# Four early loads of v asked for at other points, with a new list of priority offsets, in a gated linear attention followed by a four-expert layer

## The chip, the core and the metric

The kernel runs on one core of a Trainium2 chip. Its engines are TensorE (PE in the profile; PEld is its weight load), VectorE (DVE), ScalarE (ACT), GpSimd (POOL) and SyncE (SP). SP and POOL also ask for DMA transfers, and the core's 16 DMA engines carry them. The metric is device time in microseconds (us) of one execution, as a median of several runs.

## The reference

Two stages. The first is a linear attention with a forget gate: for each of 4 batches and 8 heads a 48 x 48 state is decayed and updated over 768 steps, and read with q. The second takes the 3072 rows of 384 numbers that come out and runs four experts over all of them, each a 384 -> 1024 -> 384 layer with relu, weighted by normalised probabilities.

```python
f = 1.0 / (1.0 + np.exp(-f_logit))
for t in range(S):                                   # S = 768
    state = f[:, :, t, :, None] * state + np.einsum('bhd,bhe->bhde', k[:, :, t], v[:, :, t])
    y[:, :, t] = np.einsum('bhd,bhde->bhe', q[:, :, t], state)
x = y.transpose(0, 2, 1, 3).reshape(3072, 384)
p = probs / (probs.sum(-1, keepdims=True) + 1e-09)
for e in range(4):
    out += p[:, e:e + 1] * (np.maximum(x @ w1[e], 0.0) @ w2[e])
```

## The kernel before

**Tiling.** The 768 steps are cut into six chunks c of 128 steps. A chunk has four batches b. For each (c, b) the attention part runs these steps, which carry these names in the kernel's planner: `ld f`, `ld k`, `ld q`, `ld v` (loads from HBM), `gate1`, `gate2` (ACT: log of the gate), `cs` (PE: running sum of it over the 128 steps, line 319), `exps` (ACT, line 339), `q` and `k` (products with the exponentials on DVE or POOL, line 347), `tpq`, `tpk` (transposes on PE for the first batches, line 356; DMA transposes `tp`, line 360, later), `ev_tp` (eviction of those), `at` (PE, line 383), `ev_at0`, `ev_at1` (DVE, masked eviction, line 387), `y` (PE, lines 394 and 398; needs v), then `ev_y`, `xt`, `ev_xt` in the first chunk and part of the second (eviction, transpose on PE, eviction: x ready for the experts), or `ev_ys` (ACT or DVE, lines 370 and 372: the eviction scaled by two experts' probabilities) and the DMA transpose `xs` (line 375) later. `kv`, `ev_kv` and `sf` (lines 404, 411, 416, 419) update the state.

The expert part of chunk 0 and half of chunk 1 is written plainly: `h c.e.fc` (PE, x times w1, line 432), `relu`, `o` (PE, h times w2, line 447), `ev_o`. From the second half of chunk 1 on, two experts and two batches make one group c.hf.p: eight `hs` steps (PE, line 464), their `relu_s`, four sums `s1` to `s4` (DVE, line 482), and seven products `p` (PE, line 501) in place of eight, each with its eviction `ev_p` (DVE or ACT, line 509). `store` writes the output.

**Order.** Nothing is scheduled by a compiler. Every step is put into a planner (`Plan`, line 53) with the engines that could run it and a cost there, a due time (`prio`), what it depends on, and the buffers that it takes and frees. The planner lays the steps out with a list scheduler, and the instructions of each engine are emitted in that order; each engine then runs its list strictly in order. `MOVES` (line 15) is a list of offsets that are added to the due times of single steps, with `@DVE` or `@ACT` where a step is tied to one engine. Before the first expert matmul the planner also puts idle matmuls on a tile of ones (`pad`, line 867) between PE's steps, as many as its plan has room for.

**The first loads.** The sixteen loads of chunk 0 are one batch each. f, k and q go through SP's queue (line 282). v is asked for by POOL (line 278), since its load also casts to bf16. POOL's list in this stretch also holds one or more of the `q` and `k` products and the eleven loads of the experts' weights (`w issue`, line 291). w 0 and w 1 are the two halves of w1 of expert 0, w 2 and w 3 those of expert 1, w 4 and w 5 the halves of w2 of expert 0, and w 6 to w 10 whole matrices. A v issue can be gated: `after` (line 258) makes it wait until a given load has landed. `v_gate` names the gates, and the planner is told the same dependency:

```python
    v_gate, issued = [(0, "k", 1), (0, "k", 2)], []
...
    for i, x in enumerate("f0 k0 q0 f1 k1 q1 f2 f3 k2 q2 v0 k3 q3 v1 v2".split()):
```

The string sets the due times of the loads on the DMA engines; v 0.3 is added behind the first weight load. So before the change v 0.0 waits for k 0.1, v 0.1 waits for k 0.2, and v 0.2 and v 0.3 follow in POOL's list without a gate.

Of the kernel before, what the change touches and what calls it, by code (L numbers as in the profile page):

```python
# [12 lines left out]


MOVES = (
    "q 0.2=3.2;k 0.3=-8.9;ev_y 0.3=-23.3@ACT;cs 1.0=0.8;k 1.0=-0.2;cs 1.1=-4.4;v 1.2=8@ACT;tp 1.2=-43.6;tp 1.3=-25;ev_xt 1.1=24.3;"
    "xs 1.3.1=7.9;ld v2.2=7.4;h 0.0.0.0=-7.3;relu 0.0.0.0=3.1@DVE;relu 0.0.2.0=10.6;relu 0.0.3.0=29@ACT;h 0.0.5.0=6.8;h 0.1.1.0=-16.7;"
    "h 0.1.2.0=-22.6;h 0.1.3.0=-119.1;o 0.1.1.1=4.2;o 0.1.3.0=11.3;h 0.3.2.0=-3.7;relu 0.3.3.0=-13.8@DVE;h 0.3.4.0=-12.9;o 0.2.2.0=28.6;"
    "o 0.2.3.0=-1.9;h 0.3.7.0=39.5;cs 2.1=31.3;tp 2.2=9.1;ev_at1 2.0=17;ev_ys 2.0.0.1=-0@ACT;ev_ys 2.1.1.0=-35.5@ACT;xs 2.1.1=12.6;"
    "ev_ys 2.2.0.1=-0.6@ACT;kv 2.2=48.1;ld k3.0=-2.9;o 0.3.2.1=2.1;store 0.3.0=22.7;h 1.0.0.0=-9.5;relu 1.0.4.0=-0.8@DVE;"  # L20
    "h 1.0.5.0=-42.9;h 1.1.0.0=-50.1;h 1.1.1.0=-41.2;h 1.1.2.0=-4;relu 1.1.2.0=-12.9@DVE;h 1.1.3.0=-41;h 1.1.4.0=-2.3;"
    "relu 1.1.6.0=-44.9@DVE;h 1.2.0.0=-1.9;h 1.2.1.0=-7.4;h 1.2.3.0=-7.1;relu 1.2.4.0=1.6@DVE;h 1.2.5.0=8.6;h 1.3.2.0=8;o 1.2.1.0=10.2;"
    "h 1.3.4.0=-11.3;h 1.3.5.0=-23.7;h 1.3.6.0=-11.9;hs 1.1.0.1.4=-1.2;relu_s 1.1.0.1.4=-9@ACT;hs 1.1.0.1.6=-6.4;hs 1.1.1.1.4=4.8;"
    "exps 3.0=7.9;k 3.1=-3.6;k 3.2=56.5;ev_ys 3.0.0.0=-1.5@DVE;ev_ys 3.0.0.1=0@ACT;ev_ys 3.0.1.0=44.9;ev_ys 3.1.0.0=50.8@DVE;"
    "ev_ys 3.1.0.1=0@ACT;ev_at1 3.2=7.6;ev_ys 3.3.1.0=0.1@DVE;ev_ys 3.3.1.1=6.1@DVE;ev_kv 3.0=23;kv 3.3=9.3;ev_kv 3.3=13.2;"
    "ld q4.0=-11.2;ld k4.2=26.7;ld q4.2=26.5;ev_p 1.1.1.1=6.4;hs 2.0.0.0.2=4.5;p 1.1.1.3=8.6;store 1.2.0=34.8;hs 2.0.0.0.6=-14.7;"
    "hs 2.0.0.1.6=2.4;s3 2.0.0=-32.1;hs 2.0.1.1.0=6.1;hs 2.0.1.0.4=-4.2;hs 2.0.1.1.4=2.8;relu_s 2.0.1.1.4=51.5;p 2.0.1.7=2.6;"
    "p 2.0.1.3=33.7;ev_p 2.0.1.4=-10.5;p 2.1.0.1=1.3;p 2.1.0.2=1.7;hs 2.1.1.0.2=-1.4;hs 2.1.1.1.2=-3.1;p 2.1.0.5=-17.1;"
    "hs 2.1.1.0.6=27.4;hs 2.1.1.1.6=-5.3;s2 2.1.1=-16.6;gate2 4.0=33.9;cs 4.0=-2.3;v 4.1=-8;ev_ys 4.0.0.0=5.6@DVE;ev_ys 4.0.0.1=44@DVE;"
    "xs 4.0.0=-37.1;ev_ys 4.0.1.0=-0@ACT;ev_at1 4.1=1.9;y 4.1=-4.7;ev_ys 4.1.0.1=3.8@DVE;ev_at0 4.3=-29.9;ev_ys 4.3.1.0=-16.5;"  # L30
    "ev_kv 4.1=-1.3;kv 4.2=15.9;ld q5.0=-19.7;ld v5.0=8.7;ld k5.2=25;relu_s 3.0.0.1.0=0.4@DVE;p 2.1.1.6=11.2;ev_p 2.1.1.5=-1.2;"
    "hs 3.0.0.0.4=3.6;relu_s 3.0.0.0.4=8.9@ACT;hs 3.0.0.1.6=-4.9;p 3.0.0.2=3.2;hs 3.0.1.0.2=-1.1;relu_s 3.0.1.0.2=42.4;p 3.0.0.5=-25.6;"
    "p 3.0.0.7=2.1;s3 3.0.1=27.4;hs 3.1.0.1.0=11.9;ev_p 3.0.1.2=13.5;relu_s 3.1.0.1.6=-19.4@ACT;hs 3.1.1.1.0=-27.5;ev_p 3.1.0.2=-4;"
    "hs 3.1.1.1.2=7.5;hs 3.1.1.1.4=-1.8;hs 3.1.1.0.6=-24.3;cs 5.2=-7;cs 5.3=13.5;ev_ys 5.1.0.0=-15;hs 4.0.0.0.0=2.9;"
    "relu_s 4.0.0.0.0=-27.5@DVE;ev_p 3.1.1.1=-15.6;hs 4.0.0.0.2=20.6;p 3.1.1.5=-4.7;hs 4.0.0.1.4=-17.4;hs 4.0.0.1.6=-20.2;"
    "ev_p 4.0.0.3=25.5;s3 4.0.1=-0.4;hs 4.1.1.1.4=16.2;hs 5.0.0.1.2=-13.7;s4 5.0.0=-8.4;hs 5.1.0.1.6=1.5;hs 5.1.1.0.2=-4.8;"
    "hs 5.1.1.1.2=-1.9;relu_s 5.1.1.1.4=-21.2@DVE;s2 5.1.1=14.5"
)


# [98 lines left out]
def kernel(  # L139
# [105 lines left out]
    def tl(kind, *key):  # L245

        if (kind, key) not in tiles:
            room = alias.get(kind, kind if kind in rooms else "ps_m" if kind in inbank else "ps_m")
            slot = P.slot[(room,) + key if kind == room else (room, kind) + key]
            if room in ("gp", "qk", "e"):  # L250
                tiles[kind, key] = pads[room, slot]
            else:
                shape, dt = shapes[kind]
                pool = ps if room.startswith("ps_") else wk
                tiles[kind, key] = pool.tile(shape, dt, name=f"{room}{slot}")
        return tiles[kind, key]

    def after(later, earlier):
        tc.add_manual_dep(later.ins, earlier.ins.name,
                          mybir.DependencyInfo(mybir.DependencyClass.Sync, mybir.DependencyReason.DATA),  # L260
                          reason="order of transfers")
# [4 lines left out]
    def hh(b, n=1):  # L266
        return slice((b % 2) * H, (b % 2 + n) * H)
# [8 lines left out]
    def load(c, nm, b, n):  # L276
        if (c, nm) == (0, "v"):
            ins[c, nm, b] = nc.gpsimd.dma_start(out=tl("vb", c, b), in_=srcs[nm][c, :, b * H:(b + n) * H, :])  # L278
            if b < 2:
                after(ins[c, nm, b], ins[v_gate[b]])  # L280
            return
        ins[c, nm, b] = nc.sync.dma_start(out=tl(nm, c, b // 2)[:, hh(b, n), :],  # L282
                                          in_=srcs[nm][c, :, b * H:(b + n) * H, :])
        if (c, nm, b) == (1, "f", 0):
            after(ins[c, nm, b], ins["w", 6])
        if (c, nm, b) == (1, "f", 1):
            after(ins[c, nm, b], ins["w", w_gate])
# [228 lines left out]
    ld = {}  # L516
    def add_load(c, nm, b, n, prio, deps=(), cost=None):
        op = P.add(f"ld {nm}{c}.{b}", {"DMA": cost or (1.05 if c else 1.1) * n}, lambda e: load(c, nm, b, n), prio,
                   deps=deps, takes=[(nm, c, b // 2)], lag=2.0)
        for i in range(n):  # L520
            ld[c, nm, b + i] = op
        return op


    v_gate, issued = [(0, "k", 1), (0, "k", 2)], []

    def add_v(b, prio):
        issued.append(P.add(f"v issue {b}", {"POOL": 0.8}, lambda _: load(0, "v", b, 1), -600 + b,
                            deps=issued[-1:] + ([ld[v_gate[b]]] if b < 2 else []), takes=[("vb", 0, b)], lag=1.2))
        ld[0, "v", b] = P.add(f"ld v0.{b}", {"DMA": 1.1}, lambda _: None, prio, deps=issued[-1:], lag=2.0)  # L530

    for i, x in enumerate("f0 k0 q0 f1 k1 q1 f2 f3 k2 q2 v0 k3 q3 v1 v2".split()):
        nm, b = x[0], int(x[1])
        if nm == "v":
            add_v(b, -1000 + i)
        else:
            add_load(0, nm, b, 1, -1000 + i)
# [148 lines left out]
    def add_o(c, e, nt, half):  # L686
        p = unit[0] + 0.5
        by_cols = (c, e, nt) == (C - 1, E - 1, B - 1)
        part = half if by_cols else 0
        cols = slice(half * Din // 2, (half + 1) * Din // 2) if by_cols else slice(0, Din)  # L690
        fcs = range(KF) if by_cols else range(half * 4, half * 4 + 4)
        key = ("ps_m", "op", c, e, nt, part)
        d = [hdone[k] for k in hdone if k[:2] == (c, e) and k[2] in fcs and k[3] <= nt * T]
        m = omm[c, e, nt] = P.add(f"o {c}.{e}.{nt}.{half}", {"PE": 0.645}, lambda _: mm_o(c, e, nt, fcs, part, cols), p,
                                  deps=d + (wd[e, 2] if by_cols or len(wd[e, 2]) == 1 else [wd[e, 2][half]]) + [omm.get((c, e, nt))], takes=[key], lag=0.2, frees=[("h", c, e, half_of(c, nt * T))])
        if half == 1 or by_cols:
            w = 0.36 if by_cols else 0.62
            ev = oev[c, e, nt] = P.add(f"ev_o {c}.{e}.{nt}.{part}", {"ACT": 0.58, "DVE": 0.56} if e == 0 else {"DVE": w},
                                       lambda g: ev_o(c, e, nt, part, cols, g), p - 1,
                                       deps=[m, oev.get((c, e - 1, nt)), pdone], takes=[("o", c, nt // 2)], frees=[key])  # L700
            if e == E - 1:
                P.add(f"store {c}.{nt}.{part}", {"DMA": 0.6}, lambda _: store(c, nt, cols), p - 25, deps=[ev], frees=[("o", c, nt // 2)], lag=2.0)
# [32 lines left out]
    def zip_groups(hg, pg, os=()):  # L735
# [73 lines left out]
        for i in range(8):  # L809
            h_unit(i)  # L810
            if i < len(os):
                add_o(*os[i])
            if i == LAG and pg is not None:
                todo.extend((pg, i) for i in range(7))
# [57 lines left out]
YP, RP = 17, 50  # L872
B1, S1, B2, S2 = -10, 4, -2, 6
LAG = 0


# [28 lines left out]
```

## Time and profile before

| what | value |
|---|---|
| median of 3 runs | 289.33 us (289.2 to 290.66) |
| the profiled execution's own time | 289.56 us |
| span of its profile | 287.8 us |
| TensorE's granted clock | 1.00 throughout |
| PE busy | 279.7 us, 97% of the span |
| DVE, ACT, POOL busy | 193.4, 182.7, 114.6 us |
| start of the first expert matmul (line 432) | 19.85 us |
| the ten first weight loads asked for by POOL | from 14.38 us on |

The span counts from the first instruction to the last, and the execution's own time has 1.76 us around it. A profile row reads: start, duration, engine, line, operation, what it writes and reads, how many; in brackets how long the engine sat idle before it and what ended that. The chain of work that ended last goes back from the last instruction to what released it, and so on to the start; "issue" in it is time in which the engine waited for nothing that the profile shows.

### The profile page before, as it was taken

The page shows a single profiled execution, that of the slowest core. Times are in us where ns is not written, and L with a number is a line of the kernel's source. Part 1 is how long each engine was busy: PE and PEld are TensorE (multiplying, and loading weights), DVE is VectorE, ACT ScalarE, POOL GpSimd, SP SyncE. Part 2 cuts the span into 40 slices and gives each one's busy share as a digit, 9 for nine tenths or more (in the row PEclk, how much of TensorE's full clock was granted, in tenths as well). Part 3 has the DMA queues.
Part 4 walks back from the last instruction along what each step waited for, and adds up shares of the span by engine and source line. Part 5 has one row for each costly group of instructions (what it writes and reads, how often), then busy time and mean ns, then how long its engine had stood idle before and what let it go on. Part 6 is the DMA issues. An engine that isn't in the chain of part 4 may idle for free.

```text
span 287.8 us, 7401 instructions
## 1 busy us (share of the span) xinstructions
PE 279.7 (97%) x2982; PEld 234.3 (81%) x2982; DVE 193.4 (67%) x383; ACT 182.7 (63%) x348; POOL 114.6 (40%) x182
## 2 busy tenths in 40 slices
PE   7989999999999999999999999999999999999994
PEld 2566555567776999999999999999989999999994
DVE  4665232798799758875888879787758830885283
ACT  5857656757766867866676757757657258643630
POOL 5694800429392841678267247306630002000000
PEclk9999999999999999999999999999999999999999
DMA  8999999998979999998999999999374212071101
GB/s 161 199 140 202 208 199 201 185 217 196 176 141 158 188 186 191 169 202 187 184 161 168 175 198 187 197 193 170 63 128 70 44 55 39 6 107 57 56 2 55
DMA packets 157782, 41.85 MB, mean 145 GB/s; under 512 B 148124, under 2 KB 156956, under 8 KB 157748
## 3 DMA queue, kind: packets, MB, share of 16 engines
q1 hardware_dynamic: 146500, 34.66, 65.2%
q0 software_dynamic: 11248, 6.72, 16.8%
q8 instruction: 23, 0.38, 0.5%
q14 instruction: 11, 0.09, 0.1%
HBM read 31.51 MB, written 4.72 MB: 126 GB/s over the span
## 4 chain that ended last, share of the span: by engine, by line
PE 87%; DMA 5%; POOL 2%; SPq 2%; DVE 1%; issue 1%; ACT 0%; DVEq 0%
PE ps_m L464 33%; PE ps_m L501 29%; PE ps_m L432 10%; PE ps_m L447 8%; SPq L282 2%; DMA w_sb<-in_moe_w_dram 2%; PE ps_m L383 2%; DMA x<-yb 1%; DMA k<-in_k_dram 1%; PE ps_m L398 1%; POOL qk L347 1%; PE ps_m L394 1%; PE ps_m L404 1%; PE ps_m L319 1%; POOL vb L278 1%
## 5 line engine op out<-in xcount | busy, mean ns | idle before, releaser
L464 PE MATMUL ps_m<-x,w_sb 128*128 128x256 bf16 x864 | 106.8, 273 | 0.5 <-DMA x<-yb 0.5
L472 ACT ACTIVATE h<-ps_m 128x512 bf16<-128x512 f32 x116 | 69.0, 597 | 45.3 <-PE ps_m L464 41.6
L464 PEld LDWEIGHTS <-w_sb 128*128 128x128 bf16 x864 | 82.6, 98 | 9.5 <-PE ps_m L383 0.6
L509 DVE TENSOR_TENSOR o<-ps_m,o 128x192 f32<-128x192 f32 x91 | 31.5, 354 | 29.5 <-PE ps_m L501 28.1
L501 PEld LDWEIGHTS <-S 128*128 128x128 bf16 x576 | 48.7, 98 | 0.9
L347 POOL TENSOR_TENSOR qk<-q,e 128x384 bf16<-128x384 f32 x20 | 24.4, 1225 | 35.6 <-ACT e L339 34.3
L432 PE MATMUL ps_m<-x,w_sb 128*128 128x256 bf16 (+3 forms) x228 | 36.0, 301 | 1.6 <-DMA w_sb<-in_moe_w_dram 1.3
L501 PEld LDWEIGHTS <-h 128*128 128x128 bf16 x432 | 36.1, 98 | 1.0
L447 PE MATMUL ps_m<-w_sb,h 128*128 128x384 bf16 x192 | 36.3, 326 | 0.0
L482 DVE TENSOR_TENSOR S<-h 128x1024 bf16<-128x1024 bf16 x36 | 25.5, 733 | 13.3 <-ACT h L472 13.3
L419 POOL TENSOR_TENSOR Sf<-Sf,egs 48x192 f32<-48x192 f32 x40 | 20.4, 511 | 31.8 <-DVE Sf L411 25.0
L387 DVE TENSOR_TENSOR AT<-ps_m,mask 128x512 bf16<-128x512 f32 x48 | 30.3, 682 | 3.4 <-PE ps_m L383 3.4
L443 ACT ACTIVATE h<-ps_m 128x512 bf16<-128x512 f32 (+2 forms) x43 | 21.7, 514 | 14.5 <-PE ps_m L432 12.9
L339 ACT ACTIVATE e<-ps_m 128x384 f32<-128x384 f32 x48 | 26.7, 671 | 6.0 <-PE ps_m L319 4.0
L432 PEld LDWEIGHTS <-w_sb 128*128 128x128 bf16 x228 | 20.3, 98 | 11.3 <-DMA w_sb<-in_moe_w_dram 1.8
L501 PE MATMUL ps_m<-ts_sb,S 128*128 128x192 bf16 x288 | 28.8, 246 | 0.0
L501 PE MATMUL ps_m<-w_sb,S 128*128 128x192 bf16 x288 | 28.7, 246 | 0.0
L447 PEld LDWEIGHTS <-h 128*128 128x128 bf16 x192 | 18.4, 98 | 12.2
L501 PE MATMUL ps_m<-w_sb,h 128*128 128x192 bf16 x288 | 27.9, 246 | 0.0
L370 ACT ACTIVATE yb<-ps_m,pn 128x384 bf16<-128x384 f32 x49 | 25.7, 586 | 0.6 <-DVE yb L372 0.4
L271 ACT COPY o<-ps_m 128x192 f32<-128x192 f32 x35 | 11.2, 319 | 21.5 <-PE ps_m L501 21.0
L347 POOL TENSOR_TENSOR qk<-k,e 128x384 bf16<-128x384 f32 x19 | 19.9, 1046 | 11.9 <-ACT e L339 6.3
(74 smaller groups left out, 322.2 us busy)
## 6 DMA issues: line engine op xcount, KB each, us to landing
out_dram<-o SPq DMA_DIRECT2D x23, 192.0 KB, 2.2
w_sb<-in_moe_w_dram POOLq DMA_DIRECT2D x5, 768.0 KB, 17.8
k<-in_k_dram SPq DMA_DIRECT2D x10, 384.0 KB, 6.0
q<-in_q_dram SPq DMA_DIRECT2D x10, 384.0 KB, 5.9
v<-in_v_dram SPq DMA_DIRECT2D x10, 384.0 KB, 5.5
f<-in_f_logit_dram SPq DMA_DIRECT2D x9, 384.0 KB, 4.3
w_sb<-in_moe_w_dram POOLq DMA_DIRECT2D x6, 384.0 KB, 8.2
f<-in_f_logit_dram SPq DMA_DIRECT2D x6, 192.0 KB, 4.0
```

The costliest lines, as they stand in the source:

```text
L339: nc.scalar.activation(out=o, in_=i, func=AF.Exp, scale=1.0 if j else -1.0)
L347: engines[eng].tensor_tensor(out=tl("qk", c, b)[:, j, :, 0:D].rearrange("t (i r) d -> t i r d", r=2), in0=tl("qk"[j], c, b // 2)[:, hh(b), ...
L370: nc.scalar.activation(out=ys, in_=y, func=AF.Copy, scale=pe)
L387: nc.vector.tensor_tensor(out=tl("AT", c, b)[:, r].rearrange("s i t -> s (i t)"), in0=tl("A", c, b, r).rearrange("s i t -> s (i t)"), in1= ...
L432: nc.tensor.matmul(out=hp(c, e, fc, n0, n1, nf)[:, f], lhsT=w1_sb[:, e, kk, (fc + f) * 128:(fc + f + 1) * 128], rhs=tl("xT", c)[:, kk, n0: ...
L443: nc.scalar.activation(out=dst, in_=src, func=AF.Relu)
L447: nc.tensor.matmul(out=tl("op", c, e, nt, part)[:, cols], lhsT=tl("h", c, e, half_of(c, nt * T))[:, fc, nt * T:(nt + 1) * T], rhs=w2_sb[:, ...
L464: nc.tensor.matmul(out=out_[:, f], lhsT=w1_sb[:, e, kk, (fc + f) * 128:(fc + f + 1) * 128], rhs=tl("xs", c, hf, p)[:, el, kk, :], start=(k ...
L472: nc.scalar.activation(out=dst, in_=tl("hp", c, hf, p, el, fc), func=AF.Relu)
L482: nc.vector.tensor_tensor(out=s(j), in0=in0, in1=in1, op=op)
L501: nc.tensor.matmul(out=out_, lhsT=lhs[:, fc, :], rhs=rhs[:, fc, :], start=(first and fc == 0), stop=(fc == KF - 1), skip_group_check=True)
L509: nc.vector.tensor_tensor(out=o, in0=src, in1=o, op=ALU.add)
```

## The change

Three things. The order string and the gates become two names at the end of the file. In the string, v 0.0 stands ahead of f 0.3, v 0.1 ahead of q 0.2 and v 0.2 ahead of k 0.3. And v 0.0 now waits for q 0.1, v 0.1 for f 0.3, v 0.2 for k 0.2; v 0.3 keeps its place and has no gate. The whole list `MOVES` is another one, so that the planner lays out nearly all later work in another order too.

```diff
 MOVES = (
-    "q 0.2=3.2;k 0.3=-8.9;ev_y 0.3=-23.3@ACT;cs 1.0=0.8;k 1.0=-0.2;cs 1.1=-4.4;v 1.2=8@ACT;tp 1.2=-43.6;tp 1.3=-25;ev_xt 1.1=24.3;"
...
+    "q 0.2=38.4@DVE;ev_y 0.1=0@ACT;ev_y 0.2=11.5@ACT;cs 1.0=28.2;k 1.2=-44.2;v 1.2=14.2@ACT;exps 1.3=-34.5;k 1.3=-2.4;ev_y 1.1=0@DVE;"
...
     def load(c, nm, b, n):
         if (c, nm) == (0, "v"):
             ins[c, nm, b] = nc.gpsimd.dma_start(out=tl("vb", c, b), in_=srcs[nm][c, :, b * H:(b + n) * H, :])
-            if b < 2:
+            if b < len(v_gate):
                 after(ins[c, nm, b], ins[v_gate[b]])
             return
...
-    v_gate, issued = [(0, "k", 1), (0, "k", 2)], []
+    v_gate, issued = VG, []
...
-                            deps=issued[-1:] + ([ld[v_gate[b]]] if b < 2 else []), takes=[("vb", 0, b)], lag=1.2))
+                            deps=issued[-1:] + ([ld[v_gate[b]]] if b < len(v_gate) else []), takes=[("vb", 0, b)], lag=1.2))
...
-    for i, x in enumerate("f0 k0 q0 f1 k1 q1 f2 f3 k2 q2 v0 k3 q3 v1 v2".split()):
+    for i, x in enumerate(ORDER.split()):
...
+ORDER = "f0 k0 q0 f1 k1 q1 f2 v0 f3 k2 v1 q2 v2 k3 q3"
+VG = [(0, "q", 1), (0, "f", 3), (0, "k", 2)]
```

What comes out as the engines' lists in the first stretch, by the two built programs:

| engine | before | after |
|---|---|---|
| POOL | k 0.0, v 0.0, q 0.1, v 0.1, v 0.2, q 0.2, w 0, v 0.3, w 1 to w 9 | k 0.0, v 0.0, q 0.1, v 0.1, v 0.2, w 0, v 0.3, w 1 to w 9 |
| SP | ... k 0.2, q 0.2, ld p, k 0.3, q 0.3 | ... k 0.2, ld p, q 0.2, k 0.3, q 0.3 |
| DVE | ... k 0.2, ev_at0 0.1, k 0.3, ev_at1 0.1, ev_xt 0.0, q 0.3, ev_at 0.2, ev_at 0.3 | ... k 0.2, q 0.2, ev_at0 0.1, ev_at1 0.1, k 0.3, q 0.3, ev_at 0.2, ev_at 0.3 |
| PE | ... at 0.1, y 0.0, tpk 0.2, pp, tpq 0.2, xt 0.0, tpk 0.3, y 0.1, at 0.2, tpq 0.3, xt 0.1, at 0.3, h 0.0.0.0, y 0.2, ... | ... pp, tpk 0.2, at 0.1, y 0.0, tpq 0.2, xt 0.0, at 0.2, tpk 0.3, y 0.1, tpq 0.3, xt 0.1, y 0.2, at 0.3, h 0.0.0.0, ... |

`ld p` and `pp` are the load of the probabilities and its transpose on PE. The number of idle matmuls is 36 in both.

## The prediction

> **What bounds the kernel now.** I read the page's busy times first, then the chain of work by time, then PE's timeline, then the DMA engines in windows of 1 us. The page:
>
> ```profile
> PE 279.7 (97%) x2982; PEld 234.3 (81%) x2982; DVE 193.4 (67%) x383; ACT 182.7 (63%) x348; POOL 114.6 (40%) x182
> ```
>
> PE is the bound, and its matmuls are the same ones after the change. So time can only come from PE's idle stretches, or go into new ones. The chain shows what lies ahead of PE's first expert matmul:
>
> ```profile
> 7.22 4.08 DMA k<-in_k_dram
> 11.30 0.30 issue
> 11.60 1.44 POOL vb L278 x2
> 13.04 0.39 issue
> 13.43 0.95 POOL qk L347
> 14.38 5.42 DMA w_sb<-in_moe_w_dram
> 19.80 0.05 issue
> 19.85 0.50 PE ps_m L432 x3
> ```
>
> k 0.2 lands at 11.30; POOL, which had waited for it, asks for v 0.1 and v 0.2, does the product q 0.2, asks for w 0 at 14.38; w 0 lands at 19.80. PE's timeline shows what PE loses:
>
> ```profile
> 19.85 0.50 PE L432 MATMUL ps_m<-x,w_sb 128*128 128x256 bf16 x3 [1.30 <-DMA w_sb<-in_moe_w_dram]
> 22.15 0.83 PE L432 MATMUL ps_m<-x,w_sb 128*128 128x128 bf16 x12 [0.25 <-DVE x L273]
> 22.98 3.65 PE L432 MATMUL ps_m<-x,w_sb 128*128 128x384 bf16 x18
> ...
> 29.62 2.76 PE L447 MATMUL ps_m<-w_sb,h 128*128 128x384 bf16 x16
> ```
>
> The brackets are idle time. Going through the rest of this timeline I find one more of any size, 0.48 us at 91.77 before the first `hs`, released by a DMA transpose (x<-yb). Elsewhere PE starts the next matmul as soon as its stream allows, apart from the same 0.1 us at each turn to and from line 383. So little is left to win: 1.30 + 0.25 + 0.48 = 2.03 us, 0.7% of the time.
>
> **The change at the start.** *POOL.* q 0.1 is asked for at 4.45 and lands at 8.2, f 0.3 at 10.3, k 0.2 at 11.3 (the landings in the trace; a gated issue starts 0.3 later, as at 11.30 to 11.60). An issue takes 0.9 us on POOL (0.93 median), a product 1.02 there. New list: v 0.0 at 8.5 (it was 7.79), q 0.1 at 9.5 (was 8.88), v 0.1 at 10.6 (was 11.60), v 0.2 at 11.6 (was 12.54), w 0 at 12.5. That is 1.9 us ahead of 14.38: 1.0 because the product q 0.2 has left POOL's list, 0.9 because v 0.1 is issued in POOL's idle time before k 0.2 lands. All weight issues behind w 0 move with it, v 0.3 too. With the old 5.42 us to landing w 0 would be there at 17.9.
>
> *The DMA engines.* The windows give share (1.00 or more is full; requests overlap) and GB/s in the last two columns:
>
> ```profile
> 10.00:11.00 1.00, 0.82 (x11) 0.47 (x10) 1.00 (x3) 0.97 (x3) 0.00 (x0) 1.00 2.00 147
> 15.00:16.00 1.00, 1.00 (x14) 0.77 (x13) 0.98 (x3) 0.68 (x1) 1.00 (x2) 1.00 1.40 78
> 16.00:17.00 1.00, 1.00 (x19) 0.62 (x18) 0.31 (x1) 1.00 (x3) 1.00 (x3) 1.00 0.80 57
> 17.00:18.00 1.00, 1.00 (x14) 0.64 (x10) 0.90 (x2) 0.82 (x3) 1.00 (x2) 1.00 1.27 190
> 20.00:21.00 1.00, 1.00 (x17) 0.92 (x16) 0.42 (x1) 0.42 (x2) 1.00 (x2) 1.00 1.28 205
> ```
>
> They are full except from 15 to 17: 57 GB/s where weights move at 190 to 205 (v counts half, since bf16 is written). There the queue had run dry until w 0's request was written: some 1.0 us lost. The early w 0 fills that. But v 0.0's burst, which fills 10 to 11 now, comes 0.7 later, while SP now asks for q 0.2 behind the load of the probabilities (0.77 us of SP's queue), so that some 0.6 us at 10 to 10.7 goes empty. The weights as a stream come earlier by about 1.0 - 0.6 = 0.4 us, at most by the 1.0, at worst not at all. w 0 itself comes earlier by more, since it no longer stands last: about 18.2.
>
> The Trainium skill, DMA: Bandwidth & Descriptors, section "Issuing engines are not separate DMA queues", says that transfers asked for by different engines run on the same 16 DMA engines and interleave, and that asking from several saves only issue time. The share of 2.00 at 10 to 11, where v shares with SP's loads, agrees; by the rule alone the gain would be only the filled gap, 0.4 us, and by POOL's list alone the whole 1.3 us.
>
> *The other engines.* q 0.2 now runs on DVE, 0.55 us (its row there) in place of 1.02 on POOL, but between k 0.2 and ev_at0 0.1, and it waits for q 0.2's load. That landed at 13.0 and is now 0.77 us of SP's queue later, beside v 0.1: I take 13.4, with 14.9 (where the last load, q 0.3, landed) as the late end. Behind it wait ev_at0 0.1 and ev_at1 0.1 (0.69 each), k 0.3 and q 0.3 (0.6 and 0.55), the four evictions of b 2 and 3. Step by step with the durations of before: q 0.2 13.7 to 14.25, ev_at0/1 0.1 to 15.7, tpq 0.2 at 14.4, xt 0.0 behind three idle matmuls (0.216 each) 15.4, ev_tp 0.2 on ACT to 15.9, at 0.2 behind three more 16.4, k 0.3 and q 0.3 (loads 15.2 and 16) to 17.0, tpk 0.3 16.8, y 0.1 17.0 (its row: 16.38), ev_y 0.1 to 18.2, four idle matmuls, xt 0.1 18.4, ev_xt 0.1 to 19.3, y 0.2 18.8, at 0.3 18.9. First `h` at 19.5: **the wait for w 0 goes, and x 0.1, until now 1.4 us early, is what ends last.** But y 0.2 and at 0.3 are already done then, and PE runs on: four `h`, xt 0.2, y 0.3 (behind DVE's ev_at 0.3) 21.1, the two narrow `h` 21.3 to 22.0. The first matmul of 384 columns, 22.98 before, comes at 22.0; it has both xt 0.3 (0.34 us) still to do, so 0.65 is won.
>
> *What catches it.* The next step that needs new weights is o 0.0.0.1 (w 5, which landed at 30.78; its first matmul, third of the four steps from 29.62, at 30.92: 0.14 of slack). With the weights 0.4 earlier it can move by 0.54. w 10 (59.61, first use 60.32) leaves 0.7. **Taken for the start: -0.55**; ends: -1.55 (both idle stretches gone, weights keep up) and +0.8 (q 0.2's load at 14.9: 1.5 later, of which the 0.65 covers part).
>
> **The change behind the start.** About a third of PE's steps stand elsewhere. I compare, in both orders, the PE work that lies between a step and the next that needs it, at PE's rates (0.66 us for an `hs` or a `p`, 0.65 for an `o`). Nearly all of these covers are as long as before or longer, and where they shrink they stay long (group 3.1.0: 9 us after y 3.3, from 21). Thinner are three:
>
> - xt 1.0 to the first `h` of chunk 1: 1.6 us of work before, 0.8 after, to cover one eviction (0.4 to 0.5) and its hand-overs: +0.1, at most +0.5.
> - y 5.2 to the first `hs` of group 5.1.0: 8.9 before, 7.6 after. The transposes between them:
>
> ```profile
> 250.44 6.23 SPq L375 DMA_TRANSPOSE x<-yb  x4
> DMA to landing us min/median/max: 2.7/2.8/4.8
> ```
>
>   y 5.2 ends at 248.75; the third transpose, the one needed, is issued two pitches of 1.3 later than 250.44, at 253.1, and lands 2.8 later at 255.9, or at 257.9 with the longest. PE would be there at 248.75 + 7.6 = 256.35: +0.1, at most +1.5.
> - The last seven products: p 5.1.1.7 follows p 5.1.1.6, whose eviction into the same bank it needs (0.36 on DVE and two hand-overs), with one `p` between instead of two: +0.1, at most +0.2.
>
> The wait of 0.48 at 91.77 has the same covers (9.4 and 7.6 us) in both orders: kept. The moves between ACT and DVE cost nothing while PE is busy 97% and they 67% and 63% (the page); if a product's DVE sums come late, an `s` step (0.73) is the price of one. **Taken: +0.3**, ends -0.5 and +2.5.
>
> **Sum.** Against the profiled execution: 289.56 - 0.55 + 0.3 = 289.31. The median of the runs stands 0.23 below the profiled one: 289.1.
>
> **The rivals.**
>
> *The weights keep up* (0.15). Speaks for it: the empty 15 to 17. Against: q 0.2's later load, and 0.14 of slack at w 5. Price: 289.33 - 1.55, and up to 0.5 more at 91.77: 287.3 to 287.8.
>
> *DVE waits for q 0.2* (0.2). In DVE's list a product with a late load now stands ahead of all later evictions. Speaks for it: SP's queue, and the full DMA engines at 11 to 14; against: 0.65 us in hand. Price: up to +0.8 and the +0.3: 289.3 to 290.4. It includes the case that the change moves nothing: a wait for x 0.1 or w 5 in the place of that for w 0.
>
> *Thin covers break* (0.17): the side of slower. One mechanism: the DMA transposes of line 375 landing late in the order of the new list. Its place: the first `hs` of groups 5.1.0 (7.6 us behind y 5.2) and 5.0.0 (7.2 behind y 5.1, 7.9 before), and 4.1.0 (8.1, from 14.5). It decides where a landing takes over 3.3 us instead of 2.8 in the first; the longest, 4.8, costs 1.5 there and about 1 in each of the others. Two or three of them: 289.1 + 2 to 289.1 + 3, so 290.9 to 292. Against: in the quiet end of the kernel few DMAs run beside (the page's GB/s at 6 to 107 there).
>
> *My forecast* (0.48): 288.4 to 289.8.
>
> **Numbers.** About 0.5% (1.45 us: under 287.9 or over 290.8) is what a measurement of this kernel can tell from no change. Faster by more: the first rival, 0.15. Slower by more: the third, 0.17, and a little of the second, 0.18 in all. Same: 0.67. The range leaves out the far half of each outer rival: 287.6 to 291.2.
>
> **What would show it.** Right: w 0 asked for at about 12.5 and landing by 18.5; the first `h` at 19.3 to 19.8, released by ACT's x (line 271) and no longer by w_sb; the first matmul of 384 columns at 22.0; o 0.0.0.1 released by w 5 or nearly so. Wrong: w 0 landing after 19; DVE idle before the product of line 347 until after 14; idle PE of over 0.5 us before a first `hs` of chunks 3 to 5. The forecast falls if PE's idle time behind 30 us is over 1.5 us.

## The result and the profile after

The changed kernel takes 290.9 us (median of 13 runs, 290.35 to 291.31), the kernel before on the same chip 289.81 (13 runs, 289.2 to 290.66): ratio 1.0033, 95% interval 1.0021 to 1.0046. It is slower by about 1.0 us, less than the 0.5% of the prediction, but on the other side of zero from the -0.25 forecast. The profiled span is 289.1 us in place of 287.8. Line numbers are 3 lower than before (432 is 429, 464 is 461, 482 is 479). The profiled execution of one later run (e10, 295.35 us at a granted clock of 0.988) was a slow one and is left out of all readings of traces.

The page's busy times, the chain at the start, and PE's timeline (all its rows with 0.2 us or more of idle time behind 12 us, and the row that ends with the first 384-column matmuls; it shows the shape of the narrow ones ahead of them, and they start at 22.05):

```profile
PE 280.3 (97%) x2982; PEld 234.1 (81%) x2982; DVE 200.0 (69%) x385; ACT 182.9 (63%) x347; POOL 117.7 (41%) x181
```

```profile
5.32 3.79 DMA f<-in_f_logit_dram
...
9.68 1.29 POOL qk L344
10.98 1.76 POOL vb L275 x2
12.74 6.77 DMA w_sb<-in_moe_w_dram
```

```profile
19.56 0.83 PE L429 MATMUL ps_m<-x,w_sb 128*128 128x256 bf16 x6 [0.20 <-DMA w_sb<-in_moe_w_dram]
...
21.25 1.46 PE L429 MATMUL ps_m<-x,w_sb 128*128 128x128 bf16 x15
...
91.54 3.44 PE L461 MATMUL ps_m<-x,w_sb 128*128 128x256 bf16 x30 [1.13 <-DMA x<-yb]
181.97 0.33 PE L401 MATMUL ps_m<-vb,qk 128*128 128x96 bf16 x4 [0.26 <-ACT h L469]
202.08 0.83 PE L498 MATMUL ps_m<-ts_sb,S 128*128 128x192 bf16 x8 [0.44 <-DVE S L479]
```

DVE's busy time grew by 6.6 us although it runs only two instructions more. At the start the wait of 1.30 for w 0 shrank to 0.20; before the first `hs` 0.48 became 1.13; and two stretches stand where there was none. A row hides gaps between its own matmuls, so I also compared each pair of neighbouring matmuls with the usual distance of its kind: the new gaps behind 150 us are 0.30 at 157.1, 0.23 at 179.9, 0.42 at 181.4 and 0.60 at 201.4, 1.55 in all.

The account, after against before: o 0.0.0.1, the first step on w 5, starts at 30.09 in place of 30.92, **-0.83**; the first `hs` at 91.54 in place of 91.77, so 0.6 of that is lost at the wait; the four gaps **+1.55**. -0.23 + 1.55 = 1.32; the spans differ by 1.30.

What stands behind the gaps is on DVE. The chain of work that ended last leaves PE there and runs through these pieces (the `h` at 156.80 stands in DVE's list behind two sums that took 2.64 together; the ACT pieces wait for DVE's `yb`, and that for the sum):

```profile
156.80 0.69 DVE h L467
...
177.06 3.10 DVE S L479
...
181.43 0.49 ACT h L469
...
199.88 2.16 DVE S L479
```

VectorE's and then GpSimd's rows around 178 us:

```profile
177.06 3.11 DVE L479 TENSOR_TENSOR S<-h 128x1024 bf16<-128x1024 bf16 x1
```

```profile
176.72 0.50 POOL L416 TENSOR_TENSOR Sf<-Sf,egs 48x192 f32<-48x192 f32 x1 [0.45 <-DVE Sf L408]
177.18 1.19 POOL L344 TENSOR_TENSOR qk<-q,e 128x384 bf16<-128x384 f32 x1
178.33 0.33 POOL L413 CAST sb<-Sf 48x192 bf16<-48x192 f32 x1
178.63 0.98 POOL L344 TENSOR_TENSOR qk<-k,e 128x384 bf16<-128x384 f32 x1
179.69 0.84 POOL L416 TENSOR_TENSOR Sf<-Sf,egs 48x192 f32<-48x192 f32 x1
```

A sum `S` takes 0.68 us undisturbed; this one took 3.11, while POOL ran its list without a break. The three groups of the sums' line, min/median/max ns, after and then before:

```profile
L479 DVE TENSOR_TENSOR S<-h x36: 678/686/3110, 99.7 to 279.5; 128x1024 bf16<-128x1024 bf16 x36
L479 DVE TENSOR_TENSOR S<-S,h x18: 674/684/989, 101.6 to 280.1; 128x1024 bf16<-128x1024 bf16 x18
L479 DVE TENSOR_TENSOR S<-h,S x18: 674/691/1979, 102.8 to 281.0; 128x1024 bf16<-128x1024 bf16 x18
```

```profile
L482 DVE TENSOR_TENSOR S<-h x36: 681/685/1164, 101.0 to 277.5; 128x1024 bf16<-128x1024 bf16 x36
L482 DVE TENSOR_TENSOR S<-S,h x18: 681/684/1343, 102.6 to 279.3; 128x1024 bf16<-128x1024 bf16 x18
L482 DVE TENSOR_TENSOR S<-h,S x18: 681/684/1684, 103.6 to 280.1; 128x1024 bf16<-128x1024 bf16 x18
```

The medians are the same, the longest are not. Before, some sums were long too, but PE waited for none of them. What the 72 sums take beyond 0.683 us each adds up to 10.7 us after and 4.9 before: 5.8 of the 6.6 us by which DVE's busy time grew. The products `p` need the sum; the evictions `yb` and `h` stand behind it in DVE's list.

**Theory:** the start gains; the new order behind it loses, because it puts DVE's sums beside POOL's products, which hold them up. **Rivals:** (1) the earlier start itself makes the later waits, whatever the order; (2) DVE's new order is at fault by itself, and the long sums only fill waiting time; (3) any work on POOL holds the sums up, not that with two inputs.

### The profile page after: what moved, and what is told of

Read it like the earlier page. It is cut to its first block, busy times and chain, and to the rows that moved or that the text cites. A ratio compares the mean times of both kernels' runs of the same rounds, so it can differ in the third digit from the quotient of the medians.

```text
span 289.1 us, 7391 instructions
## 1 busy us (share of the span) xinstructions
PE 280.3 (97%) x2982; PEld 234.1 (81%) x2982; DVE 200.0 (69%) x385; ACT 182.9 (63%) x347; POOL 117.7 (41%) x181
## 4 chain that ended last, share of the span: by engine, by line
PE 86%; DMA 5%; DVE 4%; SPq 1%; POOL 1%; ACT 1%; issue 0%; DVEq 0%
PE ps_m L461 31%; PE ps_m L498 27%; PE ps_m L429 11%; PE ps_m L444 10%; DMA w_sb<-in_moe_w_dram 2%; DVE S L479 2%; PE ps_m L380 2%; DMA x<-yb 2%; SPq L279 1%; PE ps_m L395 1%; DMA f<-in_f_logit_dram 1%; PE ps_m L391 1%; PE ps_m L401 1%; PE ps_m L316 1%; DVE h L467 1%; DVE yb L369 1%
## 5 line engine op out<-in xcount | busy, mean ns | idle before, releaser
L479 DVE TENSOR_TENSOR S<-h 128x1024 bf16<-128x1024 bf16 x36 | 30.7, 884 | 10.9 <-ACT h L469 10.9
L416 POOL TENSOR_TENSOR Sf<-Sf,egs 48x192 f32<-48x192 f32 x40 | 23.4, 585 | 31.0 <-DVE Sf L408 21.7
L440 ACT ACTIVATE h<-ps_m 128x512 bf16<-128x512 f32 (+2 forms) x50 | 23.9, 494 | 13.0 <-PE ps_m L429 12.2
L444 PEld LDWEIGHTS <-h 128*128 128x128 bf16 x192 | 18.5, 98 | 12.5
L467 DVE TENSOR_SCALAR h<-ps_m 128x512 bf16<-128x512 f32 x28 | 19.1, 689 | 8.6 <-PE ps_m L461 5.9
```

The lines of the kernel that those rows point to most:

```text
L440: nc.scalar.activation(out=dst, in_=src, func=AF.Relu)
L444: nc.tensor.matmul(out=tl("op", c, e, nt, part)[:, cols], lhsT=tl("h", c, e, half_of(c, nt * T))[:, fc, nt * T:(nt + 1) * T], rhs=w2_sb[:, ...
L479: nc.vector.tensor_tensor(out=s(j), in0=in0, in1=in1, op=op)
```

## The experiments

In most of them the planner is replaced by a written list of its steps (engine, step, start, end, idle matmuls ahead), laid out in that order: `P.replay(LISTED)` for `P.run()`. At the planner's 42.2 and 140 us both orders have done the same set of steps, so a list can follow one order up to there and the other behind it. Each ratio is to the kernel before on the same chip.

**e1: the new start, the old order behind it.** Gates, loads and order of the change up to the planner's 42.2 us, then the list of before.

```diff
-    done = P.run()
+    done = P.replay(LISTED)
```

> The changed kernel's gates, loads and steps up to the planner's 42.2 us (where both orders have done the same set of steps), then the steps of the kernel before in its own order. Theory 1: the start wins about 0.85 us and the new offsets behind it lose 2.2 us (1.55 in four idle stretches of PE at 157 to 202, 0.66 at 90). Then this kernel is faster than before by 0.2 (if x for the first hs lands at the same 91.5 us as in both traces, so that the wait there eats the rest) to 0.85: ratio 0.997 to 0.9993. Rival 2: the earlier start itself collides with later transfers and makes the waits behind it: then the new idle stretches appear here too and it is slower than before by about 1 us (ratio 1.003).

288.86 us, ratio 0.9948 (0.993 to 0.9965): faster than both kernels, and by more than was expected: 1.5 us by the ratio, with the kernel before at 290.18 there in the median. First expert matmul 19.46; nothing idle behind 91 us; no sum of `S<-h` over 1.08 us (of the line's other sums up to 1.69, as before). Rival 1 falls: the earlier start costs nothing later but part of the wait at 90:

```profile
90.21 0.40 PE L391 MATMUL ps_m<-QK 48*128 48x128 bf16 x8 [0.27 <-DMA QK<-qk]
90.98 2.78 PE L472 MATMUL ps_m<-x,w_sb 128*128 128x256 bf16 x24 [0.38 <-DMA x<-yb]
```

**e2: the old start, the new order behind it.** The other way round.

```diff
-ORDER = "f0 k0 q0 f1 k1 q1 f2 v0 f3 k2 v1 q2 v2 k3 q3"
-VG = [(0, "q", 1), (0, "f", 3), (0, "k", 2)]
+ORDER = "f0 k0 q0 f1 k1 q1 f2 f3 k2 q2 v0 k3 q3 v1 v2"
+VG = [(0, "k", 1), (0, "k", 2)]
```

> The kernel before up to the planner's 42.2 us with its gates, then the changed kernel's order. Theory 1: none of the start's gain and all of the loss: slower than before by 1.5 to 2.2 us, ratio 1.005 to 1.0075. Rival 2 (the earlier start makes the waits): about as before, ratio 0.999 to 1.001.

292.8 us, ratio 1.0081 (1.0054 to 1.0109), with the four gaps again (0.58, 0.46, 0.42, 0.58 at 159 to 204) and a sum of 3.33 us. The order behind the start is what loses: 2.4 us by the ratio, again more than expected. The two halves add up to 0.9 us, about what the changed kernel lost (1.0), so following a written list shifts nothing by itself that shows here.

**e3: the change up to the planner's 140 us, then the list of before.** The edit is that of e1 with the later seam.

> The changed kernel up to the planner's 140.1 us (chunk 3 begins), then the order of before. Theory 1: the four idle stretches at 157 to 202 go, 1.55 us less than the changed kernel, -0.2 to -0.5 against before: ratio 0.998 to 1.000. Rival 2: the stretches stay, ratio 1.003.

289.39 us, ratio 0.9974 (0.9954 to 0.9993). The four gaps are gone, the longest `S<-h` is 1.07 us (of the other sums 1.42), the wait at 90 stays (0.81 in its row). From the first expert matmul to PE's last it takes 263.91 us, as e1 does (263.93), and the changed kernel 265.93: from 42 to 140 the new order costs nothing. Of the 2.02 us to the changed kernel, the four gaps behind 140 are 1.55, and 0.32 is its longer wait at 91 (1.13).

**e4: thin products.** The changed kernel's order; the products of chunks 4 and 5 over one of four head pairs. It leaves out the rest of q and k there.

```diff
+        n = 1 if c >= 4 else NP
-        engines[eng].tensor_tensor(out=... , in0=... , in1=e_part(c, b, j), op=ALU.mult)
+        engines[eng].tensor_tensor(out=...[:, 0:n], in0=...[:, 0:n], in1=e_part(c, b, j)[:, 0:n], op=ALU.mult)
```

> The changed kernel with POOL's products of chunks 4 and 5 (line 344) made over a quarter of the heads; the rest of q and k is left out there, no order is changed. Theory 1a: the four idle stretches come from DVE's sums S (line 479), which take up to 3.1 us in place of 0.68 while POOL runs two-input products; with thin products the sums fall to 0.7 us each and 1.2 to 1.55 us of PE's idle time goes: ratio to before 0.998 to 1.0. Rival 1b: the new DVE order alone makes the sums late (they stand behind evictions); then the idle stretches stay, ratio 1.002 to 1.004, and S still has rows over 2 us only if something else slows it.

289.56 us, ratio 0.9969 (0.9946 to 0.9991). With DVE's order unchanged, the sum at 177 takes 0.72 us and all four gaps are gone:

```profile
176.68 0.72 DVE L491 TENSOR_TENSOR S<-h 128x1024 bf16<-128x1024 bf16 x1
```

Rival 2 falls. Rival 3 doesn't, since POOL was also less busy. (The ratio lies a little under the 0.998 expected, as in e3: the start is worth more than the pair of profiles shows.)

**e9: one input in place of two.** Whole tiles again, but each product on POOL in chunks 4 and 5 becomes two casts, one of q or k and one of e. It leaves out the product.

```diff
+        if c >= 4 and eng == "POOL":
+            nc.gpsimd.tensor_copy(out=o, in_=a)
+            nc.gpsimd.tensor_copy(out=o, in_=e_part(c, b, j))
+            return
```

> The changed kernel in its own order, with each of GpSimd's products of chunks 4 and 5 (q or k times e, 1.2 and 1.0 us) replaced by two casts of the same tile, one from q or k and one from e (0.5 us each by the rows of v's casts): the same tiles are read and written, but no instruction has two inputs. The product itself is left out there. My theory (DVE's sums are held up by GpSimd's instructions with two inputs, +0.63 us per us of overlap over 432 sums, against +0.23 for casts): the sums at 177 and 200 take 0.7 to 1.2 us in place of 3.1, the four stretches of idle PE (1.55 us in all) go or shrink below 0.4, 289.2 to 289.9, ratio 0.996 to 0.999. Rival (any work on GpSimd holds them up, and the run with thin products was quick only since GpSimd was idle): the sums still take 2 us and more, ratio 1.001 to 1.004.

289.49 us, ratio 0.9972 (0.9951 to 0.9992); no gap behind 92 us. What ran beside the sum at 177 (POOL), and the sum (DVE):

```profile
176.43 0.88 POOL L359 CAST qk<-e 128x384 bf16<-128x384 f32 x1
177.27 0.95 POOL L431 TENSOR_TENSOR Sf<-Sf,egs 48x192 f32<-48x192 f32 x1
```

```profile
176.92 0.94 DVE L494 TENSOR_TENSOR S<-h 128x1024 bf16<-128x1024 bf16 x1
```

POOL is about as busy (33.4 us between 150 and 206, 31.9 in the changed kernel), the sum takes 0.94, and the longest `S<-h` 1.28. So the long products made the long sums. That it was their two inputs is not shown: a cast is also shorter, 0.5 us for 1.0 to 1.2, and the traces speak for that. This sum ended 0.55 us behind the end of the cast at 176.43, just as sums end 0.55 behind a product (see the last section). So rival 3 holds in kind: casts hold the sums up as well, each by less.

**e5: the gates alone.** The list of before; only the three gates of the change. The product q 0.2 stays on POOL.

```diff
-VG = [(0, "k", 1), (0, "k", 2)]
+VG = [(0, "q", 1), (0, "f", 3), (0, "k", 2)]
```

> The list of before, step for step, with only the gates of the v loads changed: v 0.0 behind q 0.1, v 0.1 behind f 0.3, v 0.2 behind k 0.2 (before: k 0.1 and k 0.2). The product q 0.2 stays on POOL ahead of w 0, and SP asks for its loads in the old order. My theory: POOL's list then holds f 0.3's idle time for one issue (0.9) and no less work, so w 0 is asked for 0.6 to 0.9 earlier than 14.38, at 13.5 to 13.8, and lands at about 19.0 to 19.3 (before 19.80); first h 0.5 to 0.8 earlier, nothing new behind it: 288.9 to 289.6, ratio 0.995 to 0.998. Rival (the product's move to DVE carries the gain, since the DMA engines and not POOL's list set w 0's landing): w 0 lands within 0.2 of 19.8, ratio 0.999 to 1.001.

289.4 us, ratio 0.996 (0.9935 to 0.9985). w 0 asked for at 13.82, landed at 19.50. The time fits the theory; the landing lies between the theory's 19.0 to 19.3 and the rival's 19.6 to 20.0: the changed kernel asked 1.08 earlier, at 12.74, and had it at 19.51. PE still waits:

```profile
19.55 0.50 PE L440 MATMUL ps_m<-x,w_sb 128*128 128x256 bf16 x3 [0.88 <-DMA w_sb<-in_moe_w_dram]
```

**e6: the product q 0.2 on DVE alone.** The list and gates of before.

```diff
-POOL|q 0.2|14.5500|16.3800|0
+DVE|q 0.2|14.2000|14.6700|0
```

> The list and the gates of before, with only the product q 0.2 moved from POOL to DVE, right behind k 0.2 there. My theory: POOL loses 1.02 us ahead of w 0, so w 0 is asked for at 13.4 and lands at 18.8 to 19.5; DVE has the product at 12.9 to 13.5 (q 0.2 landed at 13.0 in before), which its idle time takes. First h 0.3 to 0.8 earlier: 288.9 to 289.7, ratio 0.995 to 0.999. Rival (the product on DVE pushes ev_at0 0.1 and all later evictions, so that x ends last): first h within 0.3 of 19.85, ratio 0.999 to 1.003.

289.77 us, ratio 0.9961 (0.9939 to 0.9984), but the profiled execution, among its slowest (290.55), doesn't show why: k 0.2 landed at 12.09 there (11.30 before), so v 0.1, v 0.2 and w 0 were asked for late, w 0 landed at 20.61, and a `y` waited 0.99 for v. DVE had the product at 13.43 and was not the hold-up. Which of the two edits carries how much stays open.

**e8: v 0.3 behind w 1.** e1 with two neighbours of POOL's list exchanged.

```diff
-POOL|v issue 3|15.1900|16.0300|0;POOL|w issue 1|16.0800|16.8800|0
+POOL|w issue 1|16.0800|16.8800|0;POOL|v issue 3|16.9300|17.7700|0
```

> The kernel of the run with the new start and the old order, with v 0.3 asked for behind w 1 instead of between w 0 and w 1. My theory: w 0 landed at 19.51 in the changed kernel, 6.77 us after it was asked for (5.42 before), because v 0.3's small pieces, asked for right behind it, ran between its own; with w 1 there instead it lands 0.5 to 1.0 earlier (18.5 to 19.0) and w 1 0.5 earlier, while v 0.3 lands about 1.5 later. First h at 18.9 to 19.3 if x 0.1 is ready. Time within 0.5 of 288.86, since w 5 or y 0.3 (which needs v 0.3) ends last behind it. Rival (w 0 shares with loads of SP's queues and v 0.1, v 0.2, which were asked for ahead of it): w 0's landing moves by less than 0.3.

289.8 us, ratio 0.9964 (0.994 to 0.9988). My theory fell, and the time lies outside the 0.5 expected: w 0 was asked for at 12.90 and landed at 19.76, no earlier. v 0.3 landed at 22.03 (19.73 in e1), and `y` 0.3 waited 0.42 for it.

**e7 and e11: the wait at 90.** e1 with the yb evictions of tile 1.3 ahead of a gate of chunk 2 on ACT, their DMA transposes ahead of `tp 2.1` in SP's queue, and three `hs` ahead of `at 2.1`. e11 is e7 once more, beside e10, which is e1 once more.

```diff
-ACT|gate1 2.2;...;ACT|ev_ys 1.3.0.0;...;DVE|ev_ys 1.3.0.1
+ACT|ev_ys 1.3.0.0;ACT|ev_ys 1.3.0.1;ACT|gate1 2.2
-DMA|tp 2.1;...;DMA|xs 1.3.0
+DMA|xs 1.3.0;DMA|tp 2.1
-PE|at 2.1;PE|hs 1.1.0.0.0;PE|hs 1.1.0.1.6;PE|hs 1.1.0.1.0
+PE|hs 1.1.0.0.0;PE|hs 1.1.0.1.6;PE|hs 1.1.0.1.0;PE|at 2.1
```

> The kernel of the run with the new start and the old order (288.86, the first hs at 90.98 behind waits of 0.45 and 0.55), with the yb evictions of tile 1.3 on ACT ahead of a gate of chunk 2, their transposes ahead of those of chunk 2 in SP's queue, and three hs ahead of the at of 2.1. My theory: the wait before the first hs stands on the transposes, which stand on ACT's list and SP's queue, and the earlier start ran into it; with both moved, the first hs comes at 89.9 or earlier and 0.6 to 1.0 of time goes: 287.8 to 288.3, ratio 0.991 to 0.994. Rival (the transposes' landing, 4 to 5 us, grows as they meet other DMAs, or chunk 2's transposes become late in their place): 288.6 to 289.4, with a new wait at the QK matmuls of chunk 2 or at hs.

> The kernel with the new start and the old order behind it once more, on the same chip as the next one, to be compared with it: ratio 0.993 to 0.9965, waits of 0.45 and 0.55 at 90.

> The kernel of the run before with the steps around the first hs moved, on the same chip. In its first profile the wait at 90 was gone (1.0 us), but x 0.1 had come 0.58 later at the start, as far as the profiled executions go by chance, and the span was the same. My theory: the start's 0.58 is chance (k 0.2 landed 0.3 later), so beside its twin this one is 0.5 to 1.0 faster: ratio 0.990 to 0.993. Rival (what is won at 90 is given back later or in the start): within 0.2 us of its twin.

e7 288.73 us, ratio 0.9933 (0.9908 to 0.9958); e11 289.3, 0.9949 (0.993 to 0.9969); e10 289.1, 0.9956 (0.9927 to 0.9985). The wait is gone in both profiles:

```profile
90.02 2.13 PE L472 MATMUL ps_m<-x,w_sb 128*128 128x256 bf16 x18
```

But the runs don't show the 0.6 to 1.0 expected: beside its twin e11 is 0.2 us slower by the medians and 0.2 faster by the ratios, and e7's and e1's intervals overlap. From the first expert matmul to PE's last, e1 takes 263.93, e7 263.32 and e11 263.56, so 0.4 to 0.6 is won, and a new gap of 0.30 at 203 gives some back. The first expert matmul came at 20.04 and 20.29 (19.46 in e1) though nothing ahead of it differs. That the start's spread alone hides the gain is argued, not shown; it stays open.

## Why the prediction was wrong, by its steps

**w 0 (wrong).** Asked for at 12.74, as predicted (12.5); landed at 19.51, not 18.2, and so past the 19 named as a sign against the forecast. The step that failed is "w 0 itself comes earlier by more, since it no longer stands last". Asked for and landed, in twelve executions:

```
old gates  14.38 -> 19.80   14.19 -> 20.61   14.92 -> 20.83
new gates  12.58 -> 19.18   12.74 -> 19.51   12.84 -> 19.66   12.90 -> 19.76
           12.93 -> 18.89   12.93 -> 19.90   13.22 -> 19.51   13.35 -> 19.49
           13.82 -> 19.50
```

With the new gates the landing doesn't follow the asking: there is no trend over 1.24 us of it. That the requests ahead have to drain first would explain it, and is argued. The Trainium skill's rule that the prediction weighed (DMA: Bandwidth & Descriptors, "Issuing engines are not separate DMA queues": only issue time is saved) had led to a gain of 0.4. The pair of profiles shows 0.29; the means of these executions lie 0.92 apart (20.41 and 19.49), for 1.46 in the asking. I had taken a value between the rule and POOL's list.

**The weights as a stream (right in the pair of profiles).** Taken 0.4 earlier; w 1 to w 4 landed 0.40 to 0.55 earlier, w 5 1.07 (29.71 for 30.78), so that w 5 left o 0.0.0.1, at 30.09, 0.38 of slack. Over the same twelve executions w 5 lies 1.47 apart (31.37 and 29.90 in the mean). The stretch from 15 to 17 is filled, as taken (by its share only 16 to 17, at 0.80, had not been full):

```profile
15.00:16.00 1.00, 1.00 (x9) 0.42 (x9) 1.00 (x3) 1.00 (x2) 1.00 (x3) 1.00 2.07 178
16.00:17.00 1.00, 1.00 (x26) 0.90 (x26) 0.90 (x3) 0.14 (x1) 1.00 (x2) 1.00 1.24 195
```

**DVE and q 0.2 (right).** Its load landed at 13.32 (taken 13.4); the product ran from 13.34. First 384-column matmul 22.05 (22.0). PE still waited 0.20 for w 0 in this execution, with x 0.1 ready at 19.02. In e1, e3, e4, e7, e9 and e11 no wait for w 0 is left: in e7, with w 0 in at 19.49, the chain runs through ACT's evictions and PE's own list to the first matmul at 20.04.

**The term "-0.55" (too small).** The pair of profiles shows -0.83, inside its ends. But the profiled execution of the kernel before (289.56) was one of its faster ones, and the new start with the old order behind it gains more over all runs: by the ratios 1.5 us in e1 and 1.3 in e10. That is near the end of -1.55, the price of the first rival.

**The wait at 91.77, "kept" (wrong).** The cover in PE's work was the same, but PE came 0.8 earlier and the transposes hardly: issued 0.89 earlier, they took 4.96 us instead of 4.30 and landed 0.23 earlier. In e1, e3 and e9 it cost 0.65, 0.81 and 0.94. A wait on something that isn't PE's work eats what PE gains ahead of it; "kept" should have been "up to the whole gain".

**The three thin covers, +0.3 (wrong).** No gap appears before the first `h` of chunk 1, before group 5.1.0 or at the last products: 0. (The 2.8 us taken for the third transpose was the median; in that profile it took 3.53 and landed at 256.62.) So the third rival, whose 290.9 to 292 holds the result, is refuted in its mechanism, though one transpose was late elsewhere.

**DVE's sums (the step that failed most).** "If a product's DVE sums come late, an `s` step (0.73) is the price of one." I priced the sum by its mean, put the moves between ACT and DVE at nothing since DVE was busy 67%, and compared only the PE work between steps. The 0.73 was itself a mixture: 0.68 undisturbed and some longer. I never asked what POOL runs beside it in the new order. e3, e4 and e9 show what stands in its place: a sum of up to 3.11 us, four gaps, 1.55 us. In e2, the new order without the new start, it comes to 2.4 us with the wait at 90, for the +0.3 taken; the end of +2.5 allowed for it, but for another cause. The prediction's own test, over 1.5 us of idle PE behind 30 us, came true: 1.13 and 1.55.

## What to carry to other kernels

When a change moves steps on one engine, lay the new lists of VectorE and GpSimd side by side, not only the bounding engine's: a VectorE sum of two SBUF tiles beside an unbroken run of GpSimd's products took over four times its time here (3.11 for 0.68). Price an instruction by its undisturbed time and its longest, with what ran beside the longest, not by its mean. A transfer asked for earlier into full DMA engines need not land earlier by as much (here 1.46 us in the asking, 0.92 in the landing, as means), and a gain at the start is safe only up to the next wait on something that did not move with it; here the new start with the old order behind it beats both kernels (0.9948 and 0.9956).

## What the runs showed of the hardware

Over 864 sums in the twelve traces read for this, the 583 with nothing beside them on POOL took 683 ns (median; longest 694), and the 14 beside DMA issues alone no longer (692). Of the other 267, 221 took over 0.70 us, and 217 of these ended 0.54 to 0.56 us behind the end of an instruction on POOL: 76 behind a q or k product, 79 behind an `Sf` multiply, 62 behind a cast, which has one input. In 207 cases that instruction was running when the sum began; in the other ten, all the sums of 2 us and more among them, it began later. So in the 207 cases the price goes by what POOL's instruction still has to run, and a product of 1.0 to 1.2 us has more of that than a cast of 0.3 to 0.5; the ten cost further turns.

The Trainium skill, SBUF — State Buffer, section "Who interferes with whom", says that a DVE instruction with two SBUF inputs contends with a GpSimd instruction that reads SBUF. Its section "SBUF: two separate sides" adds that whichever starts first holds the shared port pair for its whole instruction and that the other is fully blocked. The traces agree in kind, casts included. In the profile before, this sum began while POOL's product ran to 178.71, ended 0.55 later, and the next product on POOL then took 1.45 instead of 1.00:

```profile
178.10 1.16 DVE L482 TENSOR_TENSOR S<-h 128x1024 bf16<-128x1024 bf16 x1
```

Where they differ: the sum at 177.06 began while POOL's `Sf` ran to 177.22, and by the rule would have had its turn then. It lost this turn and the next: it ended at 180.17, again 0.55 behind the end of a product, but of the second one (k, 179.61). So the sum can lose several turns while POOL's list has no break; in e1 the one at 116.26 lost two turns to casts. When it does, the runs don't settle.

The start has a spread of its own: with the same instructions ahead of it, the first expert matmul came at 19.46 to 20.29 in seven profiled executions (the changed kernel, e1, e3, e4, e7, e9, e11). A few tenths at the start are not to be read from one profile.
